# One attention block on one core: heads interleaved in PSUM, whole-array transposes, and a wider value halo

## The chip, the cores and the metric

The kernel runs on one core of a Trainium2 chip. The metric is the device time of one execution in microseconds (us). A core has five engines that run their own instruction streams side by side and wait for each other through semaphores: TensorE (PE in the profile, with its weight loads as PEld), VectorE (DVE), ScalarE (ACT), GpSimd (POOL) and SyncE (SP), from which this kernel issues nearly all its DMAs. SBUF holds the operands in 128 partitions. PSUM holds the results of TensorE in 8 banks of 512 fp32 values per partition.

A matmul here is two instructions: a weight load of the stationary operand (`lhsT`) and the matmul proper, which streams the columns of the moving operand (`rhs`) and writes one PSUM column for each. With `tile_position=(0, 32*c)` a matmul uses only a 32-column strip of the array, and four such strips can work side by side.

## The reference, cut to what matters

Four layers on x of 2048 rows and 512 columns, 32 heads of 16: A, B, A, B. Each adds to x what its attention gives of the normalised x. A is linear attention with softmax features. B is a local dilated attention, and the change concerns the last block of the second B:

```python
def _B_ref(x, wqkv, wo):
    B, S, D = x.shape
    H = 32; Dh = D // H
    W, dil = 8, 2
    ...
    off = jnp.arange(W) * dil
    idx = pos[:, None] - off[None, :]
    ...
    logits = jnp.einsum("bhsd,bhswd->bhsw", q, kg) * scale
    logits = jnp.where(mask[None, None, :, :], logits, -1e9)
    attn = _softmax(logits, axis=-1)
    o = jnp.einsum("bhsw,bhswd->bhsd", attn, vg)
    return (lambda x, *d: x.transpose(*d))(o, 0, 2, 1, 3).reshape(B, S, D) @ wo

x = x + _B_ref(_layernorm(x, axis=-1), B_wqkv, B_wo)
```

A query at position p thus looks at the keys p, p-2, ... p-14. Even and odd positions never meet.

## The kernel before

The 2048 rows are worked on in four blocks of 512 rows (`b` = 0 to 3), and a block in four tiles of 128 rows (`t`). The program is written as small steps: each stage (for instance the projections of one block) registers closures for one engine under a key, and `run` (L1453) calls them in the order of a long hand-made list, `_ORDER`. What is called first stands first on its engine. So the order on every engine is fixed, and the change alters what a step issues, not where the step stands. A second list, `_CHOICE`, says whether an eviction from PSUM goes to VectorE or ScalarE (`copy`, L200; its rows in the profile have L202 and L204). A third, `_SLOTS`, gives each tile its buffer or its PSUM bank.

Blocks 0 to 2 of the B layers do the attention on VectorE: products of queries and shifted keys (`prod`, L1042), sums over the head by TensorE (`lgt`, L1049), exponentials on ScalarE (`ex`, L1056), the denominators (`den`, `rd`), the weights of the values (`pt`, L1077), products with shifted values (`pav`, L1104) and their sums by TensorE (`mo`, L1113). The results `oT` are multiplied with the output weights `WoB` (`s_out`: `mm`, L542, sometimes with x added by TensorE, L545) and evicted together with the residual (`res`, L552 on ScalarE, L555 on VectorE).

The last block, (L, b) = (1, 3), does it on TensorE instead, and while it runs, block 2 of the same layer is still in work. Its stages:

- `s_e1` (L1161) projects queries, keys and values. The keys and values of the 64 rows before the block, the halo, come from the last tile of block 2: `hk` for the keys and `hv` (L1192) for the values. `ehv` (L1221) evicts the value halo into the third plane of the tile `Vs`, and `vwh` (L1234) writes its 64 rows to a DRAM buffer `VD`, ahead of the block's own 512 rows (`vwr`). `vrd` (L1242) reads from there the values in chunks of 64 positions, even and odd ones apart, for 8 heads in each of four groups of 32 partitions; a 17th column of ones beside the 16 of each head yields the denominators.
- `s_e2` (L1268) forms for each of the four tiles `t` the logits of all heads (`sc`, L1277), their exponentials `ET` (`ex`, L1298) and, on VectorE, a mask (`msk`, L1303).
- `s_e3` (L1311) forms for each tile the weighted sums. `mo` issues 64 matmuls of 68 columns (`pv`, L1321): 32 with 32 stationary columns and then 32 with 8, which add the queries that reach over the chunk's edge. `e` is one of eight sets of four heads (one from each group), and `q` is the column strip (even or odd positions, first or second half). The tile `O` covers two PSUM banks; before, set `e` had the 68 neighbouring columns from 128 * (e % 4) on in bank e // 4. Then `ln` (L1337) and `rd` (L1340) form the reciprocals of the 32 denominators on ScalarE, and `nrm` (L1348) multiplies on VectorE, from PSUM to the bf16 tile `oB`.
- `s_e4` (L1356) transposes `oB` by matmuls with the identity as the moving operand (`pt`, L1365). Before, 16 matmuls to a tile, each with 32 stationary columns picked at a step of 16 from `oB`, which gathers the rows of the result in the order that `WoB` has its rows. The moving identity is read as `"p (r q) -> p q r"` with r = 2, which puts even and odd positions back in order. `pe` evicts the result into `oBT`, and the same `s_out` as above multiplies it with `WoB` and adds the residual.

The rows of `WoB` are loaded as `"(h q c) n -> c h q n"`: partition 32 * c + h of plane q holds the weight row of head h and column d = 4 * q + c of that head.

Of the kernel before, what the change touches and what calls it, by code (L numbers as in the profile page):

```python
# [11 lines left out]
ALU = mybir.AluOpType  # L12
ACT = mybir.ActivationFunctionType
# [3 lines left out]
P = 128  # L17
NJ = 16
D = 512
H = 32  # L20
DH = 16
NW = 8
HALO = 14
NB = 4
# [8 lines left out]
DV = DH + 1  # L33
# [103 lines left out]
class _Fast:  # L137
# [1023 lines left out]
    def s_e1(self, L, b):  # L1161
        nc, add = self.nc, self.step
        st = "b1_%d%d" % (L, b)
        T = {}

        def mm(i, c):
            xnT = self.xnT["B%d" % L, b]
            T[i, c] = pp = self.ps()
            for k in range(NB):
                nc.tensor.matmul(pp[:], lhsT=self.WB[:, k, i * D + c * P:i * D + (c + 1) * P], rhs=xnT[:, :, k, :],  # L1170
                                 start=(k == 0), stop=(k == NB - 1))

        def hk():
            xp = self.xnT["B%d" % L, b - 1]
            T["hk"] = pp = self.ps()
            for c in range(NB):
                for k in range(NB):
                    nc.tensor.matmul(pp[:, c * 64:(c + 1) * 64], lhsT=self.WB[:, k, D + c * P:D + (c + 1) * P],
                                     rhs=xp[:, 3, k, 64:128], start=(k == 0), stop=(k == NB - 1))

        def mv(t):
            xnT = self.xnT["B%d" % L, b]
            T[2, t] = pp = self.ps()
            for k in range(NB):
                nc.tensor.matmul(pp[:], lhsT=xnT[:, t, k, :], rhs=self.WB[:, k, 2 * D:3 * D],
                                 start=(k == 0), stop=(k == NB - 1))

        def hv():
            xp = self.xnT["B%d" % L, b - 1]
            T["hv"] = pp = self.ps()  # L1190
            for k in range(NB):
                nc.tensor.matmul(pp[0:64, :], lhsT=xp[:, 3, k, 64:128], rhs=self.WB[:, k, 2 * D:3 * D],  # L1192
                                 start=(k == 0), stop=(k == NB - 1))

        def ehk(dve):
            self.copy(dve, self.kvT[:, 0:4 * 64], T["hk"][:, 0:4 * 64])

        def vs(u):
            if ("Vs", u) not in T:
                T["Vs", u] = self.med([3, H, DV], "Vs")  # L1200
            return T["Vs", u]

        def vones(u):
            nc.gpsimd.memset(vs(u)[:, :, :, DH:DV], 1.0)

        def ev(i, c, dve):
            if i == 2:
                self.copy(dve, vs(c // 2)[:, c % 2, :, 0:DH], T[i, c][:].rearrange("p (h d) -> p h d", d=DH))
                return
            if i == 1:  # L1210
                if (L, b) not in self.K:
                    self.K[L, b] = self.med([NB, TB], "K")
                dst = self.K[L, b]
            else:
                if i not in T:
                    T[i] = self.med([NB, TB], "Qs")
                dst = T[i]
            self.copy(dve, dst[:, c, :], T[i, c][:])

        def ehv(dve):  # L1220
            self.copy(dve, vs(0)[0:64, 2, :, 0:DH], T["hv"][0:64, :].rearrange("p (h d) -> p h d", d=DH))  # L1221

        def qsc(g, i):
            lo = DH * g
            nc.sync.dma_start(out=self.Qbd[i][lo:lo + DH, :, g % 4, :], in_=T[0][lo:lo + DH, 2 * i:2 * i + 2, :])

        def vwr(u):
            if u == 0:
                self.VD[L, b] = self.dram.tile([64 + TB, H * DV], BF16, name="vd%d%d" % (L, b))
            dst = self.VD[L, b][64 + 256 * u:320 + 256 * u, :].rearrange("(t p) d -> p t d", p=P)  # L1230
            nc.sync.dma_start(out=dst, in_=vs(u)[:, 0:2, :, :].rearrange("p t h d -> p t (h d)"))

        def vwh():
            nc.sync.dma_start(out=self.VD[L, b][0:64, :], in_=vs(0)[0:64, 2, :, :].rearrange("p h d -> p (h d)"))  # L1234

        def vrd(r, j0, j1, c):
            a = self.VD[L, b][64 * j0 + r:64 * j0 + r + 1, c * 8 * DV:(c + 1) * 8 * DV]
            n = H * DV
            src = bass.AP(a.tensor, a.offset, [[2 * n, 32], [64 * n, j1 - j0], [1, 8 * DV]])
            d = self.chunk(r, j0)[32 * c:32 * c + 32, c, :]  # L1240
            dst = bass.AP(d.tensor, d.offset, [list(d.ap[0]), [VCH, j1 - j0], [1, 8 * DV]])
            nc.sync.dma_start(out=dst, in_=src)  # L1242

        add(st + "h", "PE", hk)
        self.flex(st + "h", ehk)
        for i in (1, 0):
            for c in range(NB):
                add(st + "qk"[i], "PE", mm, i, c)
                self.flex(st + "qk"[i], ev, i, c)
        for i in range(2):  # L1250
            for g in range(8):
                add(st + "q", "SP", qsc, g, i)
        for u in range(2):
            add(st + "v", "POOL", vones, u)
        add(st + "h", "PE", hv)
        self.flex(st + "h", ehv)
        for t in range(4):
            add(st + "v", "PE", mv, t)
            self.flex(st + "v", ev, 2, t)
            if t % 2:  # L1260
                add(st + "v", "SP", vwr, t // 2)
            if t == 1:
                add(st + "v", "SP", vwh)
        for r, j0, j1 in ((0, 0, 9), (1, 0, 2), (1, 2, 9)):
            for c in range(NB):
                add(st + "v", "SP", vrd, r, j0, j1, c)
# [44 lines left out]
    def s_e3(self, L, b, t):  # L1311
        nc, add = self.nc, self.step
        st = "b3_%d%d" % (L, b)
        T = {}

        def pv(e, r, s, n, pos):
            j = 1 + 2 * t + s - (pos > 0)
            E = self.ET[t if s or not pos else (t - 1) % 4]
            ks = 2 * r + (s if not pos else 1 - s)
            q = 32 * (2 * r + s)  # L1320
            nc.tensor.matmul(T["O"][q:q + n, e, 0:NB * DV], lhsT=E[:, e // 4, ks, e % 4, pos:pos + n],  # L1321
                             rhs=self.chunk(r, j)[:, :, DV * e:DV * (e + 1)],
                             start=(e % 4 == 0 and pos == 0), stop=(pos > 0),
                             tile_position=(0, q), skip_group_check=True)

        def mo():
            T["O"] = self.pp().rearrange("p o (e x) -> p (o e) x", x=P)
            for pos, n in ((0, 32), (32, 8)):
                for e in range(8):
                    for r in range(2):  # L1330
                        for s in range(2):
                            pv(e, r, s, n, pos)

        def ln():
            T["r"] = self.sm([8, NB], "rdB")
            den = T["O"][:, :, 0:NB * DV].rearrange("p e (c d) -> p e c d", d=DV)[:, :, :, DH]
            nc.scalar.activation(out=T["r"][:], in_=den, func=ACT.Ln, bias=self.tiny_t[:, 0:1])  # L1337

        def rd():
            nc.scalar.activation(out=T["r"][:], in_=T["r"][:], func=ACT.Exp, scale=-1.0,  # L1340
                                 accum_out=self.stR[:, 7 + t:8 + t])

        def nrm():
            if (L, b) not in self.oB:
                self.oB[L, b] = self.med([4, D], "oB")
            num = T["O"][:, :, 0:NB * DV].rearrange("p e (c d) -> p e c d", d=DV)[:, :, :, 0:DH]
            out = self.oB[L, b][:, t, :].rearrange("p (c e d) -> p e c d", c=NB, d=DH)
            nc.vector.tensor_tensor(out=out, in0=num, in1=T["r"][:].unsqueeze(3).to_broadcast([P, 8, NB, DH]),  # L1348
                                    op=ALU.mult)

        add(st, "PE", mo)
        add(st, "ACT", ln)
        add(st, "ACT", rd)
        add(st, "DVE", nrm)

    def s_e4(self, L, b):  # L1356
        nc, add = self.nc, self.step
        st, key = "b4_%d%d" % (L, b), "A%d" % (L + 1)
        U = {}

        def pt(t):
            U[t] = self.ps()
            for q in range(NB):
                for c in range(NB):
                    nc.tensor.matmul(U[t][32 * c:32 * c + 32, q * P:(q + 1) * P],  # L1365
                                     lhsT=self.oB[L, b][:, t, 4 * q + c::DH],
                                     rhs=self.ident[:].rearrange("p (r q) -> p q r", r=2), start=True, stop=True,
                                     tile_position=(0, 32 * c))

        def pe(t, dve):  # L1370
            if (key, b) not in self.oT:
# [725 lines left out]
```

## Time and profile before

| | |
|---|---|
| Median of 3 runs (lowest to highest) | 322.69 us (322.16 to 322.94) |
| The profiled execution's own time | 321.75 us |
| Its span, first to last instruction | 320.0 us |
| Granted TensorE clock | 0.998 of full speed |
| Busy over the span: PE, DVE, ACT, POOL | 307.5, 295.9, 274.9, 47.5 us |
| Instructions | 8889 |

A row of the profile names line, engine, operation, what is written and read (out<-in), and shapes as partitions x elements; for TensorE a pair such as 128*32 stands before the shape and gives the rows and columns of the array that are used. In rows in order of time the first two numbers are the start and the length in us from the span's start, and xN says how many instructions of one kind follow each other; a bracket gives idle time before the first of them and what ended it. Matmuls are pipelined: each lasts longer than the distance to the next, so distances of starts are what TensorE's pace is read from. "issue" is idle time without a wait that the profile shows. VectorE's rows of neighbours overlap a little for the same reason.

### The profile page before, as it was taken

How to read it: one execution, taken by the hardware profiler on the slowest of the kernel's cores; microseconds unless marked ns; L12 is line 12 of the kernel's file. 1: busy time of each engine (PE TensorE's matmuls, PEld its weight loads, DVE VectorE, ACT ScalarE, POOL GpSimd, SP SyncE). 2: the span in 40 equal slices, each digit the busy share in tenths (PEclk: the TensorE clock that was granted, in tenths of full speed). 3: DMA queues.
4: the chain of work that ended last, by engine and by line, in shares of the span. 5: the costliest groups of instructions: out<-in, count | busy, mean ns of one | idle time of the engine just before them, and what ended most of it. 6: DMA issues, size and time to landing. Idle time of an engine off the chain costs nothing. (4 is left out here: it accounts for less than half of the span.)

```text
span 320.0 us, 8889 instructions
## 1 busy us (share of the span) xinstructions
PE 307.5 (96%) x3572; PEld 152.2 (48%) x3572; DVE 295.9 (92%) x458; ACT 274.9 (86%) x638; POOL 47.5 (15%) x64
## 2 busy tenths in 40 slices
PE   7999999899999999999999999879999999999993
PEld 3554456445454444444444455544444444444541
DVE  5999996998999999999999999599997999999993
ACT  4999999999898778999999999799999777698560
POOL 6000000000004121000000000041240744035000
PEclk9999999999999999999999999999999999999999
DMA  6977100005794979948994500014389855567733
GB/s 200 349 193 148 35 2 4 2 18 148 177 160 110 152 134 142 137 83 120 153 132 54 69 0 2 4 39 113 89 171 137 151 120 126 133 159 158 182 137 103
DMA packets 45789, 36.37 MB, mean 114 GB/s; under 512 B 30832, under 2 KB 41136, under 8 KB 45744
## 3 DMA queue, kind: packets, MB, share of 16 engines
q1 hardware_dynamic: 45216, 35.75, 55.8%
q8 instruction: 29, 0.48, 0.7%
q14 instruction: 16, 0.13, 0.2%
q10 hardware_dynamic: 528, 0.02, 0.1%
HBM read 11.13 MB, written 3.25 MB: 45 GB/s over the span
## 5 line engine op out<-in xcount | busy, mean ns | idle before, releaser
L950 PE MATMUL PS<-xnT,WB 128*128 128x512 bf16 x336 | 76.8, 379 | 0.1
L1042 DVE TENSOR_TENSOR prod<-QT,K 128x4096 bf16<-128x4096 bf16 x28 | 63.4, 2286 | 0.5 <-POOL K L976 0.5
L1104 DVE TENSOR_TENSOR pav<-PT,Vg 128x4096 bf16<-128x4096 bf16 (+1 forms) x29 | 62.9, 2215 | 0.2
L950 PEld LDWEIGHTS <-WB 128*128 128x128 bf16 x336 | 37.4, 114 | 36.3 <-issue 3.3
L728 ACT ACTIVATE Eq<-PS 128x512 bf16<-128x512 f32 x64 | 36.3, 619 | 0.0
L621 ACT ACTIVATE Ek<-PS 128x512 bf16<-128x512 f32 x64 | 35.1, 622 | 0.2 <-PE PS L615 0.2
L542 PEld LDWEIGHTS <-oT 128*128 128x128 bf16 x240 | 22.3, 98 | 27.1 <-issue 1.3
L720 PE MATMUL PS<-xnT,WA 128*128 128x512 bf16 x128 | 32.0, 380 | 0.5 <-DVE s L812 0.3
L562 ACT ACTIVATE sqd<-x 128x512 bf16<-128x512 bf16 x48 | 30.0, 635 | 2.2 <-DVE x L555 2.0
L555 DVE SCALAR_TENSOR_TENSOR x<-PS,x 128x512 bf16<-128x512 f32 x47 | 30.9, 684 | 1.0 <-PE PS L542 0.9
L627 PE MATMUL PS<-WA,xnT 128*128 128x512 bf16 x128 | 31.6, 379 | 0.0
L615 PE MATMUL PS<-WA,xnT 128*128 128x512 bf16 x128 | 30.7, 379 | 0.0
L204 ACT CAST oT<-PS 128x512 bf16<-128x512 f32 (+1 forms) x50 | 26.9, 599 | 4.3 <-PE PS L1113 2.6
L542 PE MATMUL PS<-WoA,oT 128*128 128x512 bf16 x128 | 29.8, 380 | 0.0
L542 PE MATMUL PS<-WoB,oT 128*128 128x512 bf16 x112 | 27.3, 379 | 0.0
L204 ACT CAST K<-PS 128x512 bf16<-128x512 f32 x30 | 17.3, 594 | 3.0 <-PE PS L950 1.9
L615 PEld LDWEIGHTS <-xnT 128*128 128x128 bf16 x128 | 12.4, 98 | 14.8 <-issue 0.4
L627 PEld LDWEIGHTS <-xnT 128*128 128x128 bf16 x128 | 12.2, 98 | 14.5 <-issue 0.4
L673 DVE TENSOR_TENSOR Ek<-Ek,rk 128x4096 bf16<-128x4096 bf16 (+1 forms) x10 | 18.6, 1860 | 0.4 <-ACT rk L668 0.4
L720 PEld LDWEIGHTS <-WA 128*128 128x128 bf16 x128 | 11.6, 98 | 14.6 <-issue 1.7
L465 DVE TENSOR_SCALAR xn<-x,rstd,nmr 128x512 bf16<-128x512 bf16 x48 | 17.9, 420 | 0.6
L204 ACT CAST V<-PS 128x512 bf16<-128x512 f32 x26 | 15.2, 596 | 2.6 <-PE PS L950 2.6
(164 smaller groups left out, 501.2 us busy)
## 6 DMA issues: line engine op xcount, KB each, us to landing
Vg<-V SPq DMA_DIRECT2D x112, 131.5 KB, 4.3
Prho<-rd SPq DMA_DIRECT2D x8, 512.0 KB, 5.7
x<-in_A_x_dram SPq DMA_DIRECT2D x3, 512.0 KB, 6.8
WB<-in_B_wqkv_dram SPq DMA_DIRECT2D x3, 512.0 KB, 9.9
out_dram<-x SPq DMA_DIRECT2D x6, 256.0 KB, 2.5
wraw<-in_A_wqkv_dram SPq DMA_DIRECT2D x4, 256.0 KB, 4.3
vd<-Vs SPq DMA_DIRECT2D x2, 272.0 KB, 3.0
x<-in_A_x_dram SPq DMA_DIRECT2D x4, 128.0 KB, 3.6
```

Source lines behind the costliest of these rows:

```text
L204: self.nc.scalar.copy(out=out, in_=in_)
L542: nc.tensor.matmul(y[:], lhsT=lh(t, c), rhs=Wo()[:, c, :], start=(c == 0), stop=(c == NB - 1 and not onpe))
L555: nc.vector.scalar_tensor_tensor(out=xb[:, t, :], in0=T[t][:], scalar=1.0, in1=xb[:, t, :], op0=ALU.mult, op1=ALU.add, **kw)
L562: nc.scalar.activation(out=sqd[:], in_=xb[:, t, :], func=ACT.Square, accum_out=T["ss"][:, t:t + 1])
L615: nc.tensor.matmul(pk[:], lhsT=xnT[:, t, k, :], rhs=self.WA[:, k, D:2 * D], start=(k == 0), stop=(k == NB - 1))
L621: nc.scalar.activation(out=T["E"][:, t, s, :], in_=T["k", t][:], func=ACT.Exp, scale=1.0 - 2.0 * s)
L627: nc.tensor.matmul(pv[:], lhsT=xnT[:, t, k, :], rhs=self.WA[:, k, 2 * D:3 * D], start=(k == 0), stop=(k == NB - 1))
L720: nc.tensor.matmul(pq[:], lhsT=self.WA[:, k, hb * P:(hb + 1) * P], rhs=xnT[:, :, k, :], start=(k == 0), stop=(k == NB - 1))
L728: nc.scalar.activation(out=self.Eq[L, b][s][:, :, hb, :], in_=T[hb][:].rearrange("p (t i) -> p t i", t=4), func=ACT.Exp, scale=1.0 - 2.0 * s)
L950: nc.tensor.matmul(pp[:], lhsT=self.WB[:, k, i * D + c:(i + 1) * D:NB], rhs=xnT[:, :, k, :], start=(k == 0), stop=(k == NB - 1))
L1042: nc.vector.tensor_tensor(out=pr[:], in0=QT[:, c:c + 1, :].to_broadcast([P, NW, TB]), in1=win, op=ALU.mult)
L1104: nc.vector.tensor_tensor(out=pv, in0=PT[:, :, lo:lo + n].unsqueeze(1).to_broadcast([P, NB, 2, n]), in1=vw, op=ALU.mult)
```

## The change

Four things, all of them in the last block.

- In `pv` the outputs of four neighbouring sets of heads stand side by side. Column j of set e goes to word 4 * j + e % 4 of bank e // 4: the 68 columns of a matmul have a step of 4 fp32 words, and four sets interleave to 272 full words in each of the two banks.
- `ln` reads the denominators in that order, and `nrm` becomes two instructions, one for each bank, which write `oB` in the order of the rows of `WoB`: column 32 * d + h, with h = 8 * c + 4 * k + e.
- With this order, each 128 columns of `oB` are one plane of `WoB`'s rows, and `pt` becomes four matmuls with 128 stationary columns in place of sixteen with 32. The moving identity is read as before.
- The value halo is projected for all 128 rows of the last tile of block 2 in place of its last 64. The 64 rows that are wanted then lie in partitions 64 to 127 of PSUM and of `Vs`, from where they are evicted and written to DRAM.

```diff
@@ hv, ehv, vwh
-                nc.tensor.matmul(pp[0:64, :], lhsT=xp[:, 3, k, 64:128], rhs=self.WB[:, k, 2 * D:3 * D],
+                nc.tensor.matmul(pp[:], lhsT=xp[:, 3, k, :], rhs=self.WB[:, k, 2 * D:3 * D],
                                  start=(k == 0), stop=(k == NB - 1))
...
-            self.copy(dve, vs(0)[0:64, 2, :, 0:DH], T["hv"][0:64, :].rearrange("p (h d) -> p h d", d=DH))
+            self.copy(dve, vs(0)[64:P, 2, :, 0:DH], T["hv"][64:P, :].rearrange("p (h d) -> p h d", d=DH))
...
-            nc.sync.dma_start(out=self.VD[L, b][0:64, :], in_=vs(0)[0:64, 2, :, :].rearrange("p h d -> p (h d)"))
+            nc.sync.dma_start(out=self.VD[L, b][0:64, :], in_=vs(0)[64:P, 2, :, :].rearrange("p h d -> p (h d)"))
@@ pv, mo, ln, nrm
-            nc.tensor.matmul(T["O"][q:q + n, e, 0:NB * DV], lhsT=E[:, e // 4, ks, e % 4, pos:pos + n],
+            o = T["O"][q:q + n, e // 4, e % 4:e % 4 + 1]
+            out = bass.AP(o.tensor, o.offset, [list(o.ap[0]), [4, NB * DV]])
+            nc.tensor.matmul(out, lhsT=E[:, e // 4, ks, e % 4, pos:pos + n],
                              rhs=self.chunk(r, j)[:, :, DV * e:DV * (e + 1)],
                              start=(e % 4 == 0 and pos == 0), stop=(pos > 0),
                              tile_position=(0, q), skip_group_check=True)
...
-            T["O"] = self.pp().rearrange("p o (e x) -> p (o e) x", x=P)
+            T["O"] = self.pp()
...
-            T["r"] = self.sm([8, NB], "rdB")
-            den = T["O"][:, :, 0:NB * DV].rearrange("p e (c d) -> p e c d", d=DV)[:, :, :, DH]
-            nc.scalar.activation(out=T["r"][:], in_=den, func=ACT.Ln, bias=self.tiny_t[:, 0:1])
+            T["r"] = self.sm([NB, 2, 4], "rdB")
+            den = T["O"][:, :, 0:4 * NB * DV].rearrange("p k (c d e) -> p k c d e", c=NB, e=4)[:, :, :, DH]
+            nc.scalar.activation(out=T["r"][:].rearrange("p c k e -> p k c e"), in_=den, func=ACT.Ln,
+                                 bias=self.tiny_t[:, 0:1])
...
-            num = T["O"][:, :, 0:NB * DV].rearrange("p e (c d) -> p e c d", d=DV)[:, :, :, 0:DH]
-            out = self.oB[L, b][:, t, :].rearrange("p (c e d) -> p e c d", c=NB, d=DH)
-            nc.vector.tensor_tensor(out=out, in0=num, in1=T["r"][:].unsqueeze(3).to_broadcast([P, 8, NB, DH]),
-                                    op=ALU.mult)
+            for k in range(2):
+                num = T["O"][:, k, 0:4 * NB * DV].rearrange("p (c d e) -> p c d e", c=NB, e=4)[:, :, 0:DH]
+                out = self.oB[L, b][:, t, :].rearrange("p (d c k e) -> p k c d e", c=NB, k=2, e=4)[:, k]
+                rec = T["r"][:, :, k, :].unsqueeze(2).to_broadcast([P, NB, DH, 4])
+                nc.vector.tensor_tensor(out=out, in0=num, in1=rec, op=ALU.mult)
@@ pt
-            for q in range(NB):
-                for c in range(NB):
-                    nc.tensor.matmul(U[t][32 * c:32 * c + 32, q * P:(q + 1) * P],
-                                     lhsT=self.oB[L, b][:, t, 4 * q + c::DH],
-                                     rhs=self.ident[:].rearrange("p (r q) -> p q r", r=2), start=True, stop=True,
-                                     tile_position=(0, 32 * c))
+            for c in range(NB):
+                nc.tensor.matmul(U[t][:, c * P:(c + 1) * P], lhsT=self.oB[L, b][:, t, c * P:(c + 1) * P],
+                                 rhs=self.ident[:].rearrange("p (r q) -> p q r", r=2), start=True, stop=True)
```

## The prediction, made before the changed kernel was run

> **What bounds the kernel now.** I read the page first, then the busy time by stretch, then the order of time of each engine near the end. The chain of waits on the page is no help here (it keeps only the last VectorE instruction), so the bound is read from the stretch in which the changed instructions run, 292 to 312 us. The columns below are busy time and instruction count of PE, PEld, DVE, ACT and POOL, then the granted clock.
>
> ```profile
> span 320.0 us, 8889 instructions
> ...
> 292.00:297.50 5.50, 5.38 (x179) 3.12 (x168) 5.50 (x8) 4.85 (x17) 0.85 (x1) 1.00 0.84 195
> 297.50:304.90 7.40, 7.36 (x108) 3.77 (x108) 7.40 (x7) 3.44 (x9) 0.00 (x0) 1.00 0.67 170
> 304.90:310.40 5.50, 5.50 (x133) 3.11 (x132) 5.42 (x10) 3.76 (x9) 0.00 (x0) 1.00 0.50 172
> ```
>
> Two engines are full at once: DVE for 18.32 of 18.40 us, PE for 18.24. Which one can take more work is decided by their waits, and for PE those stand on its weight loads:
>
> ```profile
> 296.50 0.60 PEld L1365 LDWEIGHTS <-oB 128*32 128x32 bf16 x16
> 297.54 0.58 PEld L1321 LDWEIGHTS <-et 128*32 128x32 bf16 x64 [0.43 <-DVE et L1303]
> 298.84 0.55 PEld L542 LDWEIGHTS <-oT 128*128 128x128 bf16 x4 [0.20 <-issue]
> 304.99 0.57 PEld L1321 LDWEIGHTS <-et 128*32 128x32 bf16 x64 [0.42 <-issue]
> 307.18 0.53 PEld L1365 LDWEIGHTS <-oB 128*32 128x32 bf16 x16 [0.19 <-DVE oB L1348]
> 307.90 0.55 PEld L542 LDWEIGHTS <-oBT 128*128 128x128 bf16 x4 [0.20 <-ACT oBT L204]
> ```
>
> In this stretch PE waits for another engine only at 297.54 (the mask of the third block's exponentials) and from 307.2 on. Everything between is back to back, so TensorE time added there moves its end one for one. DVE's rows:
>
> ```profile
> 295.47 1.28 DVE L1348 TENSOR_TENSOR oB<-PS,rdB 128x512 bf16<-128x512 f32 x2
> 296.67 0.81 DVE L1303 TENSOR_TENSOR et<-et,maskW 128x1280 bf16<-128x1280 bf16 x1
> 297.40 0.68 DVE L1077 TENSOR_TENSOR PT<-E,rden 128x1024 bf16<-128x1024 bf16 x1
> 298.01 0.68 DVE L555 SCALAR_TENSOR_TENSOR x<-PS,x 128x512 bf16<-128x512 f32 x1
> ...
> 303.01 0.68 DVE L1348 TENSOR_TENSOR oB<-PS,rdB 128x512 bf16<-128x512 f32 x1
> 303.61 0.68 DVE L555 SCALAR_TENSOR_TENSOR x<-PS,x 128x512 bf16<-128x512 f32 x1
> 304.21 2.28 DVE L1104 TENSOR_TENSOR pav<-PT,Vg 128x4096 bf16<-128x4096 bf16 x1
> 306.43 0.69 DVE L1348 TENSOR_TENSOR oB<-PS,rdB 128x512 bf16<-128x512 f32 x1
> ...
> 308.14 2.36 DVE L1104 TENSOR_TENSOR pav<-PT,Vg 128x2048 bf16<-128x2048 bf16 x2
> 310.42 1.28 DVE L555 SCALAR_TENSOR_TENSOR x<-PS,x 128x512 bf16<-128x512 f32 x2
> ...
> 312.70 2.70 DVE L555 SCALAR_TENSOR_TENSOR x<-PS,x 128x512 bf16<-128x512 f32 x4 [0.55 <-PE PS L542]
> ```
>
> The last four residual adds start behind a wait for PE. The end therefore follows PE's order, and PE in turn follows DVE where it waits for it. I call the four query blocks t0 to t3; PE runs the weighted sums (L1321) of t0 and t1 early in the first stretch, of t2 at 297.54 and of t3 at 304.99, and the transposes (L1365) at 296.71, 298.07, 306.39 and just behind 307.18.
>
> **The weighted sums write with a step.** The number, shape and weights of the 256 matmuls stay, but each of the 68 columns now lands 16 bytes behind the last instead of 4. Their pace now:
>
> ```profile
> 297.54 0.21 PE L1321 MATMUL PS<-WA,et 128*32 128x68 bf16 x2 [0.16 <-DVE et L1303]
> ...
> 298.05 0.21 PE L1321 MATMUL PS<-Vx,et 128*8 128x68 bf16 x2
> 298.07 0.84 PE L1365 MATMUL PS<-ident,oB 128*32 128x128 bf16 x16
> 298.84 1.04 PE L542 MATMUL PS<-WoB,oT 128*128 128x512 bf16 x4
> ```
>
> 64 matmuls take 0.53 us, 16 groups of four column tiles at 33 ns. No output in the trace steps over elements, so the price is bounded. From below it is nothing (a gain is excluded: the same columns stream). From above I use the only TensorE stream whose neighbours lie apart, the transposes: their moving operand is the identity read as (q r), a hop of 64 elements at each column.
>
> ```profile
> L385 PEld LDWEIGHTS <-wraw x32: 95/98/99, 5.1 to 10.9; 128*128 128x128 bf16 x32
> L385 PE MATMUL PS<-ident,wraw x32: 216/219/230, 5.3 to 10.9; 128*128 128x128 bf16 x32
> ...
> L1365 PEld LDWEIGHTS <-oB x64: 135/138/162, 296.5 to 307.6; 128*32 128x32 bf16 x64
> L1365 PE MATMUL PS<-ident,oB x64: 282/285/337, 296.7 to 307.7; 128*32 128x128 bf16 x64
> ...
> 5.30 0.61 PE L385 MATMUL PS<-ident,wraw 128*128 128x128 bf16 x8
> ...
> 296.71 0.66 PE L1365 MATMUL PS<-ident,oB 128*32 128x128 bf16 x16
> ```
>
> At equal 128 columns the hopping stream takes 285 against 219 ns: 66 ns more, 0.52 ns a column. For 68 columns that is 35 ns on a stream that takes 28 at L542's pace (four in 1.04 us, of which 0.38 is the last one's own: 0.22 us for 512). A group then lasts 63 in place of 33 ns, and a block 16 x 30 = 0.48 us more. Between 0 and 0.48 I take 0.40: the hop is the nearer row, but 128 bytes on a read is the harder pattern.
>
> The Trainium skill (PSUM — Partial Sum Buffer, section Specifications (TRN2)) says that PSUM has 8-byte cachelines and that any non-contiguous access pattern slows matmuls significantly. No run here shows that yet. An estimate from that page, one column per line in place of two and so half the pace, gives 56 for 33 ns, 0.37 us a block and a sum of 1.5 in place of 1.65 us.
>
> **The transposes.** 16 column-tiled matmuls of a block become 4 whole-array ones. By the rows above, 16 take 0.66 us, of which 0.285 is the last one's own latency: four groups at 0.12 us, 0.49 in all. A whole-array matmul of 128 columns runs at 0.056 us where the identity is read straight (eight in 0.61, less 0.219, over seven). But the edit keeps the (q r) reading, and 54 ns (128 columns at L542's 0.42) + 66 are the 0.12 seen, so I expect four at 0.12: no gain, 48 fewer instructions for nothing. The bounds are 0 and 4 x (0.12 - 0.056) = 0.26 us less per block.
>
> **Changes of tile width.** PE pays when the next matmul uses another tile. At 304.68 runs a 128-column matmul, at 304.99 a 32-column one, 0.31 apart where the pace is 0.22; the weight load idles 0.42 there.
>
> ```profile
> 304.68 0.38 PE L545 MATMUL PS<-x,ident 128*128 128x512 bf16 x1
> ...
> 305.53 1.03 PE L1113 MATMUL PS<-pav,indAV 128*32 128x512 bf16 x16
> 306.39 0.67 PE L1365 MATMUL PS<-ident,oB 128*32 128x128 bf16 x16
> 306.88 0.61 PE L1113 MATMUL PS<-pav,indAV 128*32 128x512 bf16 x8
> ...
> 270.51 1.05 PE L1192 MATMUL PS<-WB,xnT 128*64 128x512 bf16 x4
> 271.59 0.58 ACT L204 CAST Vs<-PS 64x512 bf16<-64x512 f32 x1 [0.39 <-PE PS L1192]
> ```
>
> That is 0.09 a change; the way back costs as much (the last transpose of t1 starts 0.285 before 298.91, L542 at 298.84: 0.22 at a pace of 0.12). The transposes of t0 and t2 stand between 32-column neighbours (L1113 before both; L1321 and L1113 behind) and now bring two changes each: +0.19 at t0, +0.19 at t2. Those of t1 and t3 stand before L542: the change only moves.
>
> **Normalisation on DVE.** Four instructions become eight of 256 elements. The split pav shows the price of two halves: 2.36 against 2.28 us whole, 0.08. Four blocks: +0.32. Runs of four elements in place of 16 should not matter: L1348 (runs of 16 at a pitch of 17) and L555 (unbroken) both take 0.68. The logarithm on ACT still reads 32 elements. PE waits for this only at 307.18.
>
> **Value halo.** Four matmuls of 512 columns at the same pace, with 128 stationary columns. It saves one change of width (0.09), since L950 before it is 128 wide. The eviction (0.58) and the write of 64 rows only come from other partitions. This lies at 270.5, under unbroken work of DVE, which no step of the halo feeds directly:
>
> ```profile
> 265.51 6.82 DVE L1104 TENSOR_TENSOR pav<-PT,Vg 128x4096 bf16<-128x4096 bf16 x3
> 272.25 0.68 DVE L1077 TENSOR_TENSOR PT<-E,rden 128x1024 bf16<-128x1024 bf16 x1
> 272.85 8.89 DVE L1104 TENSOR_TENSOR pav<-PT,Vg 128x4096 bf16<-128x4096 bf16 x4
> ```
>
> I count nothing; if that cover were gone it would be 0.09 less.
>
> **The sum along PE.** t0 and t1: 2 x 0.40; two changes of width at t0: 0.19; together 0.99 late before 297.54. There PE had 0.33 to spare: the transposes of t0 end at 297.37, the last of them started 0.285 earlier, and 0.12 behind that start, at 297.21, PE was free. So t2 starts 0.66 late. Then 0.40 (t2), 0.40 (t3) and 0.19 (transposes of t2): 1.65. DVE is late by its 0.32 and is made to wait twice: the exponentials' denominators stand behind t0 and t1 on PE, so PT at 297.40 comes later, and the normalisation of t3 waits for its logarithm, which is 1.46 late. Queued behind that wait are the last pav halves, whose sums PE needs for the output matmuls. At the tail PE's lateness of 1.65 covers DVE's. The last residuals and the stores move with it.
>
> The profiled execution took 321.75 us, 1.75 more than its span; 321.75 + 1.65 = 323.4. It stands 0.94 under the median of the runs, 322.69, so the forecast is 322.69 + 1.65 = **324.3**. A measurement of this kernel can tell about 0.3%, 0.97 us, from no change.
>
> **Rivals.**
> - Stepping is free (price 0). Then PE loses 0.38 on widths, has 0.33 to spare, and DVE's 0.32 decides: about 323.0. For it: no row shows a stepped output that is slow. Against it: the identity read.
> - Stepping costs 0.40, but whole-array transposes run at L385's 0.056. That takes 0.26 off at t0, t1 and t2: 0.87, 323.6. For it: loads of whole tiles take 98 ns, these 139. It decides where stepping costs under 0.43: 4 x 0.43 + 0.38 - 0.33 - 0.78 is the 0.97 below.
> - The other side, not slower: stepping is free and the transposes are fast. PE is early by 0.26 a block, so the first half of pav is summed earlier at 310.4, and the split normalisation, the one added cost, is absorbed in the 0.55 us for which the last residuals wait: 322.7, no slower. It needs both prices at their lower bounds.
> - Stepping is far worse because the second half of each block adds onto what is there: 0.9 us a block or more. 4 x 0.9 + 0.38 - 0.33 = 3.65: 326.3. For it only that the matmuls of the second half accumulate; against it, that accumulating L542 keeps the full pace.
>
> **How the numbers follow.** Forecast 0.50 (prices 0.25 to 0.48: 1.05 to 1.97 us, so 323.7 to 324.7 by itself); stepping free 0.15; fast transposes 0.11; both 0.08; far worse 0.10; 0.06 for a gain that none of these names. The range runs from 322.5 (the not-slower case with the scatter of the runs) to 326.0. Slower by over 0.3%: 0.48 of the forecast, 0.04 of the fast transposes and 0.10 make 0.62. Within: 0.02 + 0.07 + 0.15 + 0.08 = 0.32. Faster: 0.06.
>
> **What would show it.** L1321's matmuls last some 30 ns longer and 64 of them take 0.9 us instead of 0.53 (wrong if 0.55). L1365's four stay 0.12 apart (wrong if 0.06), with idle weight loads before and behind them at t0 and t2. PE no longer waits for the mask of t2; DVE has a gap before PT at 297.4 and before the normalisation of t3. A pair of normalisations takes 0.76 or so in place of 0.68. If L1321 keeps its pace, the forecast is wrong.

## The result, and the profile after

| | before | after |
|---|---|---|
| Median (lowest to highest), 6 runs each | 321.93 us (320.57 to 322.94) | 324.30 us (323.65 to 324.33) |
| Ratio after to before, 95% interval | | 1.0070 (1.0053 to 1.0088) |
| Profiled execution, its span | 321.75, 320.0 us | 324.32, 322.6 us |
| Granted clock | 0.998 | 0.995 |
| Instructions | 8889 | 8797 |

The change costs 0.70%: (1.0070 - 1) x 321.93 = 2.25 us, with its interval 1.7 to 2.8. The forecast was 324.3, built as 1.65 us on top of 322.69, the median of the three runs then shown. Three more runs brought that median down to 321.93. The time is met, but the added cost is about 0.6 us larger than the sum said, and the two deviations cancel. That the forecast time came out to the digit is luck.

The first rows to read are those of the stretch that the prediction was made on. This is the busy time by stretch of the changed kernel (the stretch and its length, then PE, PEld, DVE, ACT, POOL, the granted clock, the DMA share and GB/s).

```profile
292.00:297.50 5.50, 5.08 (x154) 3.27 (x147) 5.50 (x9) 3.76 (x14) 1.11 (x1) 1.00 0.72 179
297.50:304.90 7.40, 7.40 (x104) 3.75 (x102) 6.72 (x7) 4.34 (x11) 0.00 (x0) 1.00 0.92 202
304.90:310.40 5.50, 5.50 (x106) 2.89 (x105) 4.59 (x11) 3.38 (x8) 0.00 (x0) 1.00 0.26 90
```

Before, both engines were full in all three. Now VectorE has 0.68 and 0.91 us of idle time in the second and third, and TensorE is full there: TensorE's order sets the pace. In the first stretch TensorE itself is idle for 0.42 of 5.50 us, 0.30 more than before, which the prediction did not have.

TensorE's matmuls of the changed kernel around the sums of t2 and the transposes of t0 and t1, in order of time:

```profile
298.41 0.66 PE L1368 MATMUL PS<-ident,oB 128*128 128x128 bf16 x4
299.00 0.24 PE L1323 MATMUL PS<-WA,et 128*32 128x68 bf16 x2
...
299.87 0.26 PE L1323 MATMUL PS<-WA,et 128*8 128x68 bf16 x2
...
300.07 0.66 PE L1368 MATMUL PS<-ident,oB 128*128 128x128 bf16 x4
300.57 1.02 PE L542 MATMUL PS<-WoB,oT 128*128 128x512 bf16 x4
```

From the first group of four weighted sums at 299.00 to the sixteenth at 299.87 there are 15 distances of 58 ns, where it was 33. Four whole-array transposes take 0.66 us, as 16 column-tiled ones did: 0.285 for the last and 0.12 for each before it.

The weight loads of TensorE show what it waits for:

```profile
292.11 0.10 PEld L1323 LDWEIGHTS <-et 128*32 128x32 bf16 x3
292.94 0.95 PEld L1323 LDWEIGHTS <-et 128*32 128x32 bf16 x61 [0.72 <-DMA Vx<-vd]
...
298.41 0.36 PEld L1368 LDWEIGHTS <-oB 128*128 128x128 bf16 x4 [0.42 <-DVE et L1303]
299.00 0.94 PEld L1323 LDWEIGHTS <-et 128*32 128x32 bf16 x64 [0.24 <-issue]
...
306.70 0.94 PEld L1323 LDWEIGHTS <-et 128*32 128x32 bf16 x64 [0.42 <-issue]
...
308.63 0.36 PEld L1368 LDWEIGHTS <-oB 128*128 128x128 bf16 x4 [0.42 <-issue]
309.22 0.12 PEld L1113 LDWEIGHTS <-indAV 128*32 128x32 bf16 x8 [0.24 <-issue]
309.77 0.36 PEld L1368 LDWEIGHTS <-oB 128*128 128x128 bf16 x4 [0.42 <-DVE oB L1353]
```

The idle loads ahead of and behind the transposes of t0 (298.41) and t2 (308.63) are the changes of tile width. The releaser named at 298.41 is the mask of t2, but these transposes don't read it, and the idle time is the 0.42 of every such change. New is the second row: the fourth weighted sum of t0 waits for the chunk of values `Vx` that SP fetches from `VD`. The same place before:

```profile
291.85 0.10 PEld L1321 LDWEIGHTS <-et 128*32 128x32 bf16 x3
292.12 0.65 PEld L1321 LDWEIGHTS <-et 128*32 128x32 bf16 x61 [0.17 <-issue]
```

VectorE of the changed kernel, in order of time:

```profile
289.99 2.29 DVE L1042 TENSOR_TENSOR prod<-QT,K 128x4096 bf16<-128x4096 bf16 x1
...
295.73 1.50 DVE L1353 TENSOR_TENSOR oB<-PS,rdB 128x256 bf16<-128x256 f32 x4
...
298.64 0.69 DVE L1077 TENSOR_TENSOR PT<-E,rden 128x1024 bf16<-128x1024 bf16 x1 [0.68 <-ACT rden L1072]
...
308.56 0.76 DVE L1353 TENSOR_TENSOR oB<-PS,rdB 128x256 bf16<-128x256 f32 x2 [0.77 <-ACT rdB L1343]
...
310.70 2.36 DVE L1104 TENSOR_TENSOR pav<-PT,Vg 128x2048 bf16<-128x2048 bf16 x2 [0.41 <-issue]
...
315.05 2.71 DVE L555 SCALAR_TENSOR_TENSOR x<-PS,x 128x512 bf16<-128x512 f32 x4 [0.34 <-PE PS L542]
```

The gaps of 0.68 and 0.77 us stand where the prediction put them. The third, 0.41 us ahead of the last pav halves at 310.70, it did not have. This gap stands in all seven traces of kernels that normalise in two halves, always 0.41 us, and in none of the seven of kernels that normalise in one piece, so it comes with the split or with the stepped outputs, which all seven have as well; what VectorE waits for there the profile does not show. In the changed kernel it does not reach the end: the pav halves are done at 313.06, and the last of their sums start at 313.64, behind ScalarE's eviction of the first half.

In the kernel before, the row of L1042 is this one:

```profile
289.74 2.28 DVE L1042 TENSOR_TENSOR prod<-QT,K 128x4096 bf16<-128x4096 bf16 x1
```

The changed kernel's profiled execution is thus 0.25 us late before any of the changed arithmetic in the last block; the lateness below is counted from there. The table sets the starts of the rows above against those of before, less 0.25.

| TensorE reaches | forecast late, us | measured late, us |
|---|---|---|
| the sums of t0 that read `Vx` (292.94 for 292.12) | 0 | 0.57 |
| the transposes of t0 (298.41 for 296.71) | 0.89 | 1.45 |
| the sums of t2 (299.00 for 297.54) | 0.66 | 1.21 |
| the transposes of t1 (300.07 for 298.07) | 1.06 | 1.75 |
| the output matmuls behind them (300.57 for 298.84) | 1.06 | 1.48 |
| the sums of t3 (306.70 for 304.99) | 1.06 | 1.46 |
| VectorE's last residuals (315.05 for 312.70) | 1.65 | 2.10 |

From the first row on the measured lateness stands some 0.4 to 0.7 us above the forecast, and from the output matmuls on 0.40 to 0.45: one term was missing early, and it is the first row.

### The profile page after: what moved, and what is told of

Read it like the earlier page. It is cut to its first block, busy times and chain, and to the rows that moved or that the text cites. A ratio compares the mean times of both kernels' runs of the same rounds, so it can differ in the third digit from the quotient of the medians.

```text
span 322.6 us, 8797 instructions
## 1 busy us (share of the span) xinstructions
PE 309.5 (96%) x3524; PEld 153.1 (47%) x3524; DVE 296.4 (92%) x462; ACT 275.3 (85%) x638; POOL 47.3 (15%) x64
## 5 line engine op out<-in xcount | busy, mean ns | idle before, releaser
L1042 DVE TENSOR_TENSOR prod<-QT,K 128x4096 bf16<-128x4096 bf16 x28 | 63.4, 2288 | 0.5 <-POOL K L976 0.5
```

The lines of the kernel that those rows point to most:

```text
L1042: nc.vector.tensor_tensor(out=pr[:], in0=QT[:, c:c + 1, :].to_broadcast([P, NW, TB]), in1=win, op=ALU.mult)
```

## The experiments

Ratios are to the kernel before, run beside them on the same chip, with 95% intervals; the third column is (ratio - 1) x 322 us.

| kernel | ratio | us |
|---|---|---|
| step_only | 1.0214 (1.0191 to 1.0236) | +6.9 |
| step_runs | 1.0038 (1.0026 to 1.0051) | +1.2 |
| steps_mixed | one run, 323.01 us | |
| no_step | 1.0223 (1.0190 to 1.0257) | +7.2 |
| no_step_runs | 1.0033 (1.0021 to 1.0046) | +1.1 |
| ident_copy | 1.0025 (1.0010 to 1.0040) | +0.8 |
| no_step_ident | 1.0026 (1.0015 to 1.0036) | +0.8 |
| ident_before | 0.9988 (0.9975 to 1.0001) | -0.4 |
| halo_only | 1.0004 (0.9989 to 1.0019) | +0.1 |
| changed_again | 1.0060 (1.0043 to 1.0076) | +1.9 |
| sums_later | 1.0052 (1.0038 to 1.0066) | +1.7 |
| ident_residual | 0.9984 (0.9973 to 0.9995) | -0.5 |

### The halo alone: halo_only

The edit is the three lines of `hv`, `ehv` and `vwh` on the kernel before.

> The kernel before with the value halo of 128 columns alone. Theory: the halo costs nothing, so the time is that of before within 0.3% (ratio 0.997 to 1.003), and PE waits at most 0.1 us for the chunk Vx at the weighted sums of t0. Rival: the wait of 0.72 us for the chunk Vx, which the changed kernel shows at 292.94 us and the kernel before doesn't, comes from the halo (its rows leave from partitions 64 to 127, or later); then it shows here too and the ratio is 1.0015 to 1.003 with that wait in the trace.

The time does not move, and the weight loads of the sums run through without a wait:

```profile
291.96 0.80 PEld L1321 LDWEIGHTS <-et 128*32 128x32 bf16 x64
```

The halo costs nothing that these runs can tell, and in this trace it does not bring the wait for `Vx`.

### The step alone: step_only and step_runs

Both are the kernel before with the stepped outputs. They differ in how the normalisation of one bank goes through its 256 elements:

```diff
 # step_only: four heads innermost, written 32 bytes apart
+num = T["O"][:, k, 0:4 * NB * DV].rearrange("p (c d e) -> p c d e", c=NB, e=4)[:, :, 0:DH]
+out = self.oB[L, b][:, t, :].rearrange("p (c k e d) -> p k c d e", c=NB, k=2, e=4)[:, k]
 # step_runs: one head at a time, written unbroken
+num = T["O"][:, k, 0:4 * NB * DV].rearrange("p (c d e) -> p c e d", c=NB, e=4)[:, :, :, 0:DH]
+out = self.oB[L, b][:, t, :].rearrange("p (c k e d) -> p k c e d", c=NB, k=2, e=4)[:, k]
```

> The kernel before with the stepped PSUM writes alone: weighted sums with a step of 4 words, denominators and two normalisations read accordingly, oB in the old order, 16 column-tiled transposes, halo of 64 columns. Theory: a group of four weighted sums takes 60 ns in place of 33, 64 take 0.94 us; four blocks 1.64 us less the 0.33 that PE had to spare, 1.3 us in all, ratio 1.003 to 1.0055. Rival (most of the loss comes from transposes and widths): under 0.5 us, ratio below 1.002. Rival (the step explains the whole loss, and the transposes give nothing back): ratio 1.0065 or more.

It missed by far, 6.9 us in place of 1.3. The group of its normalisations shows why, with the mean of one in ns behind the busy time:

```profile
L1353 DVE TENSOR_TENSOR oB<-PS,rdB 128x256 bf16<-128x256 f32 x8 | 9.2, 1397 | 0.4 <-ACT rdB L1343 0.4
```

256 elements take 1397 ns where the changed kernel takes 420. Only the order of the writes differs: single bf16 values 32 bytes apart, against runs of four.

> Like step_only, but the two normalisations read the stepped words head by head (16 elements, 16 bytes apart) and write oB in unbroken runs of 16, as the kernel before does; only the writes' layout is changed against step_only. Theory: in step_only VectorE paid for writes 32 bytes apart (1.2 us for 256 elements), not for the step in PSUM; here two normalisations take 0.76 us together, a group of four weighted sums 60 ns, and the time is 0.9 to 1.7 us over before, ratio 1.003 to 1.0055. Rival (reading PSUM with a step is as dear as writing with one): normalisations of 1.2 us each and ratio 1.02.

The theory held. The same view of step_runs:

```profile
L1353 DVE TENSOR_TENSOR oB<-PS,rdB 128x256 bf16<-128x256 f32 x8 | 2.9, 414 | 0.6 <-ACT rdB L1343 0.6
```

Reading with the step is free for VectorE; writing with one is not. With that out of the way the step, with the normalisation in two halves that comes with it, costs 1.2 us (0.8 to 1.6). The prediction's terms for it, 4 x 0.40 less the 0.33 to spare, make 1.27.

### The distance: steps_mixed

```diff
+STEP = {0: (1, 128), 1: (2, 69), 2: (3, 70), 3: (7, 1)}   # block: (step of a column, offset of a set), in words
+o = T["O"][q:q + n, e // 4, 0:1]
+s_, a_ = STEP[t]
+out = bass.AP(o.tensor, o.offset + a_ * (e % 4), [list(o.ap[0]), [s_, NB * DV]])
```

> The kernel before with another PSUM layout in each block: the columns of a weighted sum lie 1 word apart in t0, 2 in t1, 3 in t2 and 7 in t3, and two normalisations read them head by head. The rule of 8-byte lines (one column a line in place of two, whatever the step beyond): a group of four takes 33, 60, 60, 60 ns. Rival (the price grows with the distance): 33, then between 33 and 60 for 2 words, and more than 60 for 7. Rival (16 bytes are special): 2 and 3 words cost little.

The weight loads of the four blocks, t0 first (its first three loads stand in a row of their own):

```profile
292.21 0.57 PEld L1326 LDWEIGHTS <-et 128*32 128x32 bf16 x61 [0.20 <-issue]
...
292.96 1.15 PEld L1326 LDWEIGHTS <-et 128*32 128x32 bf16 x64
...
297.72 0.94 PEld L1326 LDWEIGHTS <-et 128*32 128x32 bf16 x64 [0.18 <-DVE et L1305]
...
305.43 0.94 PEld L1326 LDWEIGHTS <-et 128*32 128x32 bf16 x64 [0.42 <-issue]
```

With 3 and 7 words a block takes the same 0.94 us; in t1 (2 words) the loads start early behind other work, and the matmuls themselves show the pace:

```profile
293.62 0.25 PE L1326 MATMUL PS<-WA,et 128*8 128x68 bf16 x1
...
294.03 0.25 PE L1326 MATMUL PS<-WA,et 128*8 128x68 bf16 x1
```

Seven groups in 0.41 us are 59 ns each. So the steps tried, 2, 3, 4 and 7 words, all cost the same, and distance plays no part in this range.

The Trainium skill (PSUM — Partial Sum Buffer, Specifications (TRN2)) has 8-byte lines and says that any pattern with gaps slows matmuls significantly. The traces agree: half the pace, the prediction's estimate from these lines, would be 56 ns, and 58 to 59 are measured.

### The row order without the step: no_step and no_step_runs

Both are the changed kernel with the PSUM layout of before, and differ in the one normalisation of 512 elements:

```diff
 # no_step: head by head, written 64 bytes apart
+num = T["O"][:, :, 0:NB * DV].rearrange("p e (c d) -> p e c d", d=DV)[:, :, :, 0:DH]
+out = self.oB[L, b][:, t, :].rearrange("p (d c e) -> p e c d", c=NB, d=DH)
 # no_step_runs: read 512 bytes apart (reciprocals 16 bytes apart), written unbroken
+num = T["O"][:, :, 0:NB * DV].rearrange("p e (c d) -> p d c e", d=DV)[:, 0:DH]
+out = self.oB[L, b][:, t, :].rearrange("p (d c e) -> p d c e", c=NB, d=DH)
+rec = T["r"][:].rearrange("p e c -> p c e").unsqueeze(1).to_broadcast([P, DH, NB, 8])
```

> The changed kernel with neighbouring PSUM words again in the weighted sums, one normalisation of 512 elements that writes oB in the row order of WoB, whole-array transposes and halo kept. Theory (the step is the cost): a group of four weighted sums is back at 33 ns, 64 in 0.53 us; transposes stay 0.12 us apart; the normalisation takes 0.68 us, at most 0.9 if writes 64 bytes apart cost VectorE; the time is that of before plus 0 to 0.5 us, ratio 0.999 to 1.002. Rival (tile widths and the split normalisation are the cost): the ratio stays at 1.004 or above.

> Like no_step, but the normalisation reads the neighbouring words of the eight sets 512 bytes apart and writes oB in runs of 8 elements, in the row order of WoB. Theory (writes apart are dear, reads apart are not): one normalisation of 0.68 to 0.75 us; the step's 0.41 us a block is gone and the time is that of before within 0.3%, ratio 0.999 to 1.002. Rival (reads apart are dear too, so the step in PSUM was needed to have neighbours on both sides): normalisations above 2 us, ratio 1.015 or more.

Both missed, and in both it is the normalisation: writes apart in no_step, reads apart in no_step_runs, where neither the theory's 0.75 us nor the rival's 2 us came out. The normalisations of no_step, and below them those of no_step_runs:

```profile
L1348 DVE TENSOR_TENSOR oB<-PS,rdB 128x512 bf16<-128x512 f32 x4 | 9.4, 2460 | 0.0
```

```profile
L1349 DVE TENSOR_TENSOR oB<-PS,rdB 128x512 bf16<-128x512 f32 x4 | 4.1, 1066 | 0.0
```

TensorE has its 0.42 us a block back, but VectorE pays 2460 or 1066 ns where it took 684. Even the better order costs 0.38 us a block, nearly what the step costs TensorE, and on an engine that was as full. In no_step_runs two operands are read apart, the PSUM words 512 bytes and the reciprocals in SBUF 16 bytes; which of them costs the 0.38 was not tested. This is the service of the step of four: it lets the normalisation read and write four neighbours at a time, so it needs only 0.75 us.

The Trainium skill (Vector Engine (DVE) Microarchitecture Reference, Measured stream behaviour on trn2) says that an SBUF stream keeps its full rate while it comes in runs of at least two neighbouring 4-byte words that start on an 8-byte boundary. Four bf16 have the size of two such words and start on such a boundary here, and the runs of four do keep it (420 ns for 256 elements, 414 unbroken); single values 32 or 64 bytes apart fall to under a third. The page's own figures are for 4-byte elements and are not compared here.

### The hop in the moving identity: ident_copy, no_step_ident, ident_before

```diff
+# once, into PHI, which nothing reads any more
+nc.gpsimd.tensor_copy(out=self.identP.rearrange("p (q r) -> p q r", r=2),
+                      in_=self.ident[:].rearrange("p (r q) -> p q r", r=2))
-rhs=self.ident[:].rearrange("p (r q) -> p q r", r=2)
+rhs=self.identP
```

This goes on the changed kernel (ident_copy), on no_step_runs (no_step_ident) and on the kernel before (ident_before).

> The changed kernel with one addition: GpSimd copies the identity in the order (q r) once, and the transposes read this copy straight. Theory (the hop of 64 elements on the moving operand sets 0.12 us a transpose): four transposes come 0.056 us apart, each lasts 219 ns in place of 285; PE gains 0.26 us a block; the time is 0.5 to 0.8 us under the changed kernel, ratio to before 1.004 to 1.006. Rival (weight loads or the PSUM side set the pace): still 0.12 apart and ratio 1.007.

The transposes of t1 and the output matmul behind them in ident_copy:

```profile
299.98 0.40 PE L1372 MATMUL PS<-PHI,oB 128*128 128x128 bf16 x4
300.21 0.38 PE L542 MATMUL PS<-WoB,oT 128*128 128x512 bf16 x1
```

0.40 less the 0.219 of the last one leaves 0.06 for each, in place of 0.12: the hop set the pace. The profiled executions of ident_copy and of the changed kernel, both idle at `Vx` (0.95 and 0.72 us), took 323.60 and 324.32 us: 0.72 apart, and 0.78 was the prediction's figure for this rival. That the two figures are so near is in part chance, since VectorE now has a share in the end: behind its gap of 0.41 us the last pav halves are waited for.

```profile
312.76 0.27 PEld L1113 LDWEIGHTS <-indAV 128*32 128x32 bf16 x8 [0.60 <-DVE pav L1104]
```

The medians are further apart than expected, 1.0025 against 1.0070 and 1.0060, where the theory had 1.004 to 1.006; seven of ident_copy's twelve runs lie below 322.8 us, and none of the changed kernel's. The only trace is of a longer run, so why the others were shorter is not shown.

> no_step_runs with the copy of the identity in the order (q r) for the transposes. Theory: four transposes in 0.39 us in place of 0.66, PE early by 0.26 us a block less the changes of width; VectorE then decides the end, so not more than 0.5 us under before: ratio 0.997 to 1.0005. Rival (PE's order decides to the end): about 0.8 us under before, ratio 0.9975 or less.

Missed: it keeps no_step_runs' dear normalisation, and VectorE decides the end. Its last residuals follow without a wait for TensorE:

```profile
313.32 2.70 DVE L555 SCALAR_TENSOR_TENSOR x<-PS,x 128x512 bf16<-128x512 f32 x4
```

> The kernel before with nothing but the copy of the identity in the order (q r) for its 16 column-tiled transposes a block. Theory (the hop sets the pace in column tiles too): four groups at 0.056 in place of 0.12 us, 16 in 0.4 us in place of 0.66; at most 0.5 us under before, ratio 0.9975 to 1.0. Rival (the weight loads, picked at a step of 16 elements, set the pace of the column-tiled form, 135 ns against 98): still 0.12 us a group, ratio 1.000.

The 16 transposes of t2 take 0.41 us, those of t0 and t3 0.47 and 0.48, where 16 took 0.66 or 0.67:

```profile
305.86 0.41 PE L1369 MATMUL PS<-PHI,oB 128*32 128x128 bf16 x16
```

The column-tiled form gains 0.19 to 0.26 us, the whole-array form 0.26. What held the transposes was the pattern in which the identity is read, and neither the tile width nor the number of instructions. The gain in time, 0.4 us, can't be told from none.

### The wait for Vx: changed_again and sums_later

> The changed kernel once more, unedited. Theory (the wait of 0.72 us for the chunk Vx in its first trace came from where the SP queue stood in that run, and other runs are without it): the median over these runs lies 1.3 to 2.0 us over before, ratio 1.004 to 1.0062, and a trace without that wait shows the tail 1.6 us later than before. Rival (the wait belongs to the changed kernel): ratio 1.0065 to 1.008 again and the wait is there.

Neither side held fully: the ratio, 1.0060, lies within the theory's range, but the wait is there again, and the tail is late by 314.99 - 312.70 - (289.79 - 289.74) = 2.24 us.

```profile
292.88 0.94 PEld L1323 LDWEIGHTS <-et 128*32 128x32 bf16 x61 [0.88 <-DMA Vx<-vd]
```

```profile
289.79 2.29 DVE L1042 TENSOR_TENSOR prod<-QT,K 128x4096 bf16<-128x4096 bf16 x1
...
314.99 2.71 DVE L555 SCALAR_TENSOR_TENSOR x<-PS,x 128x512 bf16<-128x512 f32 x4 [0.34 <-PE PS L542]
```

The swap of sums_later moves one step of the written order:

```diff
-ig dv gt ii gt dw        # logits, sums of t0, logits
+ig dv gt gt ii dw        # logits, logits, sums of t0
```

> The changed kernel with one pair on TensorE swapped: the eight logit matmuls of block 2 that stand behind the weighted sums of t0 (0.44 us of TensorE) are issued ahead of them, so that this work covers the wait for the chunk Vx. Theory (the wait of 0.6 to 0.9 us for Vx, in both traces of the changed kernel, reaches the end, because TensorE's order decides it from there on): the idle time at Vx falls by 0.4 us, so do the output matmuls and the tail: ratio 1.0045 to 1.006, with the tail 1.9 us behind before in place of 2.3. Rival (the wait is absorbed by the slack before the mask of t2): the idle time falls, but the tail stays 2.3 us behind, ratio 1.006 to 1.007.

The loads of t0 and t1 now run through, and the tail is late by 314.10 - 312.70 - (289.52 - 289.74) = 1.62 us, near the 1.65 of the sum:

```profile
292.08 2.23 PEld L1323 LDWEIGHTS <-et 128*32 128x32 bf16 x128
```

```profile
289.52 2.28 DVE L1042 TENSOR_TENSOR prod<-QT,K 128x4096 bf16<-128x4096 bf16 x1
...
314.10 2.70 DVE L555 SCALAR_TENSOR_TENSOR x<-PS,x 128x512 bf16<-128x512 f32 x4 [0.35 <-PE PS L542]
```

In this run the fetches of `Vx` were also issued early (the row below), so the swap need not have covered all of the wait by itself.

```profile
287.95 1.85 SPq L1242 DMA_DIRECT2D Vx<-vd  x4
```

Either way, the one trace of the changed arithmetic without the wait has its tail 0.5 to 0.6 us sooner than the two with it: the wait reaches the end. The median fell too, to 1.0052, though its interval overlaps that of the changed kernel.

Where the wait comes from is less clear. The four fetches of `Vx` are the last of a row on SP. Their issue in the kernel before, in the changed one and in ident_before:

```profile
277.24 0.53 SPq L1231 DMA_DIRECT2D vd<-Vs  x1
...
287.92 1.84 SPq L1242 DMA_DIRECT2D Vx<-vd  x4
```

```profile
283.68 5.05 SPq L1242 DMA_DIRECT2D WA<-vd  x8
288.83 1.84 SPq L1242 DMA_DIRECT2D Vx<-vd  x4
```

```profile
277.17 1.49 SPq L1231 DMA_DIRECT2D vd<-Vs  x1
...
288.42 1.84 SPq L1246 DMA_DIRECT2D Vx<-vd  x4
```

In the traces of before, halo_only, step_runs, steps_mixed, ident_residual and sums_later the idle time at `Vx` is 0.20 us or none; in the changed kernel, changed_again, ident_copy, no_step, no_step_runs, no_step_ident, step_only and ident_before it is 0.55 to 1.12 (the profile names `Vx` in four of these eight, and no releaser in the others). Wherever the loads that read `Vx` have a row of their own, it starts 3.8 to 4.2 us behind the first fetch's issue: the wait follows SP.

ident_before and step_only have neither halo nor whole-array transposes, and up to the sums of t0 they run the work of the kernel before (ident_before with one copy on GpSimd more). They wait all the same. In ident_before the write of the values took 1.49 us to issue in place of 0.53, and 0.35 us of this are left at the next write (279.45 for 279.10). Such a long issue, 1.32 to 1.52 us, stands in seven of the eight traces with the wait and in none of the six without; in the eighth, the changed kernel's first, the write took 0.53 us but was issued 0.57 us later than before (277.81 for 277.24). So none of the change's parts is needed for the wait, and the long issue goes with it; what makes the issue long is not shown. All six traces with whole-array transposes in the old order have the wait, and only two of the seven others in that order; the transposes themselves run some 20 us behind that write, and whether it is chance stays open.

### A version that beats both: ident_residual

```diff
 # on ident_before: one residual add from VectorE to ScalarE, x added by TensorE
-    "100000000100101010000011...
+    "100000000110101010000011...
```

> ident_before (copied identity, columns and tiles as before) with one residual add, the one of VectorE at 303.61 us, moved to ScalarE, with x added by TensorE. Theory (VectorE is full from 292 to 312 and TensorE has 0.26 us a block to give since the transposes read straight): VectorE's later instructions start 0.3 to 0.6 us sooner and the time falls by 0.3 to 0.9 us against before, ratio 0.997 to 0.999. Rival (TensorE's order decides the tail): the 0.22 us of the added matmul is seen at the end, ratio 0.9995 to 1.001.

```profile
303.47 2.29 DVE L1104 TENSOR_TENSOR pav<-PT,Vg 128x4096 bf16<-128x4096 bf16 x1
306.14 0.69 DVE L1352 TENSOR_TENSOR oB<-PS,rdB 128x512 bf16<-128x512 f32 x1 [0.39 <-ACT rdB L1344]
...
312.10 2.71 DVE L555 SCALAR_TENSOR_TENSOR x<-PS,x 128x512 bf16<-128x512 f32 x4 [0.25 <-PE PS L542]
```

The ratio and the starts lie in the theory's range: pav starts 0.74 us sooner than in the kernel before (304.21), and the last residuals 0.60 sooner; 0.14 of both stand ahead of the changed work (L1042 at 289.60 for 289.74). At 0.9984 (0.9973 to 0.9995) it is faster than the kernel before by about 0.5 us. The copied identity alone gave 0.9988, so what the moved add brings on top of it can't be told from these times. Part of the freed time is eaten by the new wait of 0.39 for the reciprocals of t3.

## Why the prediction was right or wrong, point by point

- **The bound.** Right. TensorE's order sets the end, VectorE is made to wait before PT (0.68 us) and before the normalisation of t3 (0.77), and TensorE no longer waits for the mask of t2.
- **The stepped writes.** Right in place and size: 0.40 us a block forecast, 16 x (59 - 33) ns = 0.42 measured, and 64 matmuls in 0.94 us for the 0.9 named. The reason was the wrong one. The bound was taken from a hop in the moving operand, with a price by column that came near by chance; steps_mixed shows 59 ns for 33 from the first gap on, whatever its width, between the 56 of half the pace, which the prediction set beside its sum, and its own 63. The rivals "stepping is free" and "far worse" fall.
- **The transposes.** Right: four at 0.12 us, no gain from 16 to 4, and the identity's hop as the cause is shown by ident_copy.
- **Changes of tile width.** Right in size: from the transposes of t2 to the matmuls behind them it is 309.22 - 308.63 = 0.59 us now and was 306.88 - 306.39 = 0.49, so a change costs 0.10 for the 0.09 said. At t1 "the change only moves" left out a gain: from its transposes to the output matmuls it is 0.50 us now and was 0.77, from t2's sums to its transposes 1.07 for 0.53. That is 0.27 less and 0.54 - 0.42 = 0.12 more, so 0.15 us gained. About half of the 0.27 has nothing to do with the tiles: step_runs, with the old tiles, has 0.63 there.
- **Normalisation.** Right for the changed kernel: 0.75 to 0.76 us a pair for 0.76. The sentence that runs of four should not matter holds, but its rows (runs of 16, and unbroken) did not show the cliff behind it: single values apart cost over three times as much. The gap of 0.41 us that comes with the split or the step was left out.
- **Value halo.** Right: nothing that the runs can tell.
- **The sum.** Here a term was missing. "There PE had 0.33 to spare" and "In this stretch PE waits for another engine only at 297.54" took the arrival of `Vx` as given. The row of before at 292.12, with its 0.17 us of idle time and 4.2 us behind the first fetch's issue (287.92), already stood at that edge. With 4 x 0.02 for the dearer step and less the 0.15 gained at t1 the sum is 1.58, and sums_later, without the wait, gives 1.62. With the 0.57 us by which the changed kernel waits longer it is 2.15, against 2.10 in the trace. In the rivals, the sum 4 x 0.43 + 0.38 - 0.33 - 0.78 is 0.99 and not 0.97; nothing else hangs on it.
- **The base.** The median of three runs was 0.76 us above that of six. It hid the missing term in the absolute time, not in the ratio: 1.65 us would be 1.0051, just under the interval. The interval of changed_again, 1.0043 to 1.0076, holds 1.0051 as well, so it is the traces, and not the times alone, that show the missing term.

## What to carry to other kernels

Moving a reordering from one engine to another moves its price with it: here TensorE pays 0.42 us a block for writes with gaps, or VectorE 0.38 for reads apart, or far more for single writes apart, and the old gather in the transposes' weights cost at most 0.08 (0.41 to 0.48 us in ident_before for 0.40 in ident_copy). Before replacing many small matmuls by few large ones, see what sets their pace; here it was the order in which the moving operand was read, and one copy of it in the right order brought the 0.12 us for 128 columns down to 0.06 in one form and 0.06 to 0.09 in the other. And list what is only just in time ahead of the changed stretch, the DMAs too, since a few tenths of a microsecond of idle time in one trace can be a wait in the next.

## What the hardware showed unexpectedly

- Matmul outputs with a gap of one, two, three or six fp32 words between columns run at one and the same pace, 59 ns for 68 columns in four strips against 33 without a gap.
- VectorE reads PSUM words 4 to 28 bytes apart at full rate (in steps_mixed 1.41 us for four of 256 elements in t0 and t1, 0.76 for two in t2 and in t3), and writes single bf16 values 32 or 64 bytes apart at 1397 ns for 256 and 2460 for 512. Writes in runs of four keep the full rate (420 ns for 256). With PSUM read 512 bytes apart and the reciprocals 16 bytes apart 512 elements take 1066 ns for 684.
- A moving operand whose neighbouring columns lie 128 bytes apart takes 0.12 us for 128 columns, with whole-array and with 32-column tiles alike; read straight it takes 0.06 (0.06 to 0.09 with 32-column tiles).
